# The filter's spectrum as a stage of its own by way of DRAM, filter rows split for two t at once, scratch ordered by re/im

## The chip, the cores and the metric

One Trainium2 chip, one of its cores. The metric is the device time of one execution in microseconds. In a core TensorE (PE, with its weight loads as PEld) multiplies matrices into PSUM; VectorE (DVE), ScalarE (ACT) and GpSimd (POOL) do the elementwise work; SyncE (SP) issues most DMAs here, POOL those of the weights and of the constants. The core has 16 DMA engines. Every engine works its own queue in order and waits for others on semaphores.

## The reference

Two branches of the same normalised input are added to it, with S = 2048, D = 576, Dff = 4608, all in float32:

```python
def _A_ref(q, k, v, shift_k, ssm_k, ssm_D):
    ...
    for t in range(ks):                       # ks = 4
        k_shift = k_shift + k_pad[:, t:t + S, :] * shift_k[:, ks - 1 - t][None, None, :]
    kv = k_shift * v
    ...
    y_f = kv_f * kf_f[None, :, :, :]          # FFT of length 2 S over the sequence, per channel
    y = irfft2(y_f, ...)[:, 0, :S, :]
    y = y + kv * ssm_D[None, None, :]
    return q * y

def _B_ref(x, w1, w2):
    h = jnp.maximum(jnp.einsum("bsd,df->bsf", x, w1), 0)
    return jnp.einsum("bsf,fd->bsd", h, w2)

x = A_q
xn = _layernorm(x, axis=-1)
return x + _A_ref(xn, A_k, A_v, A_shift_k, A_ssm_k, A_ssm_D) + _B_ref(xn, B_w1, B_w2)
```

## The kernel before

**The FFN** is the larger part. It runs over two halves of the sequence (`half`), 12 chunks of 384 hidden columns (`cc`), two blocks of 512 rows (`bi`). For each, three `mm1` (L352) of 14 matmuls with 512 columns make a hidden tile; ACT (`hh`, L367) and DVE (`ll`, L368) evacuate it as a high and a low part. Four `mm2` (L371) of 2 x 9 matmuls with 288 columns follow, added to `acc` by DVE (L389, L393). Every fp32 operand is split into a high and a low part and multiplied in three passes.

**The convolution** is a transform in two steps, 2048 = 64 x 32. It is a Python generator, `conv` (L435), that emits its work in small pieces and yields a cost after each. `tick` (L753) is called twice in every `mm1` and `mm2`, with the FFN's columns as its clock, and lets the next piece be emitted when its credit allows: credit grows by `rate` (L746) times the columns. A negative yield is a pause, in which nothing is emitted until the clock has moved by so much. Thus each engine's queue holds FFN work with convolution work put between, in an order that is fixed when the kernel is built. There, `here()` (L429) ties a piece to the last `acc` and `act` instruction of the FFN, so that it is not put ahead of them.

The stages, each with a tile pool of its own:

- *Filter* (`fk`, L440). The filter is loaded as `kt`, 128 x 288 x 32 (a row holds 32 values of t for each of 288 channels). For each of the 32 columns t2, `prepare` (L460) splits `kt[:, :, t]`, read at a step of 32 elements, into `stk` for two halves of the channels. `first` (L421) multiplies each by a constant, two matmuls of 288 columns, and ACT copies the result to `z`. SP stores `z` to `zk[:, t2, :]` (L480): 128 rows of 2304 B.
- *Signal* (`fx`, L485). The same for k * v after the four taps: 32 stores to `zx` (L557).
- *Frequency* (`fm`, L560). For each of 32 groups g, 128 rows of 576 columns are loaded from `zk` and from `zx` (L572), split (L579, L580), and multiplied by the second step's matrix (`run`, L583: three matmuls of 288 columns for each half). Four copies build the filter's real and imaginary part in `k1` and `k2` (L610 to L613), two build the swapped signal `sw`; DVE multiplies and adds; the product is split again, multiplied by the inverse matrix and stored to `zy` (L648).
- *Output* (`fo`, L651). 32 loads from `zy` (L663, 128 rows each), split, the inverse of the first step, the gate with q, and the sum with `acc` (or with `fin`, the first half's result).

The scratch tensors are [128, 32, 576]: 64 x 2 frequencies and parts, t, channels. The rows that a group reads are one contiguous block. `rate` is `FFT_TOTAL`, the sum of the costs, over the FFN's columns times `SHARE` less `PAUSES` pauses. `turned_xT` (L280) turns the second half's rows for the FFN by way of `xv`, two buffers.

```python
def halves(u):
    return slice(u * A1, (u + 1) * A1), slice((1 - u) * A1, (2 - u) * A1)
```

Of the kernel before, what the change touches and what calls it, by code (L numbers as in the profile page):

```python
# [10 lines left out]
F32 = mybir.dt.float32  # L11
# [37 lines left out]
PAUSES = 16  # L49
# [7 lines left out]
FFT_TOTAL = N_FK * W_FK + N_FX * W_FX + N_FM * W_FM + N_FO * W_FO  # L57
# [18 lines left out]
def transform_constants():  # L76


    p1 = np.arange(A1)[:, None]
    f1 = np.arange(A1)[None, :]  # L80
    fwd = np.zeros((T, 2, A1, U, 2, A1, 2), np.float32)
    inv = np.zeros((T, A1, 2, U, 2, A1), np.float32)
    for t in range(T):
        for u in range(U):
            phi = 2 * np.pi * (A2 * p1 + T * u + t) * (f1 - 0.25) / S
            for c, m in enumerate((np.cos(phi), -np.sin(phi))):
                hi, lo = _split12(m)
                fwd[t, :, :, u, 0, :, c] = hi
                fwd[t, :, :, u, 1, :, c] = lo
                hi, lo = _split12(m.T / S)  # L90
                inv[t, :, c, u, u, :] = hi
                inv[t, :, c, u, 1 - u, :] = lo

    a = np.zeros((GR, 2, A2, 2, GR, A2))
    th = 2 * np.pi * np.arange(A2)[:, None] * np.arange(A2)[None, :] / A2
    for r in range(GR):
        a[r, 0, :, 0, r, :] = np.cos(th)
        a[r, 1, :, 0, r, :] = np.sin(th)
        a[r, 0, :, 1, r, :] = -np.sin(th)
        a[r, 1, :, 1, r, :] = np.cos(th)  # L100
# [8 lines left out]
def h3_ffn_kernel(ctx: ExitStack, tc, x, k, v, shift_k, ssm_k, ssm_D, w1, w2, fwd, inv, mid, out):  # L109
# [20 lines left out]
    zx = dram.tile([P, A2, D], F32, name="zx")  # L130
    zk = dram.tile([P, A2, D], F32, name="zk")
    zy = dram.tile([P, A2, D], F32, name="zy")
# [147 lines left out]
    def turned_xT(b):  # L280
# [4 lines left out]
        for c0 in range(0, 5, 2):  # L285
# [148 lines left out]

    def conv():  # L435
# [4 lines left out]
        with tc.tile_pool(name="fk", bufs=2) as fp:  # L440
            kt = fp.tile([P, NH, A2], F32, tag="kt", name="kt", bufs=1)
            skip = fp.tile([P, NH], F32, tag="skip", name="skip", bufs=1)
# [17 lines left out]
            def prepare(t, h):  # L460
                stk = fp.tile([P, NH], F32R, tag="stk", name=f"ks{t}_{h}", bufs=5)
                with here():
                    stack(stk, kt[:, :, t], h)
                return stk

            order = [T * u + t for t in range(T) for u in range(U)]
# [4 lines left out]
            for n, t2 in enumerate(order):  # L471
                stk, nxt = nxt, []
                u, t = divmod(t2, T)
                z = fp.tile([P, D], F32, tag="z", name=f"zk{t2}")
                for h in range(2):
                    first(ws[t], stk[h], z[:, h * NH:(h + 1) * NH], u)
                    if n + 1 < len(order):
                        nxt.append(prepare(order[n + 1], h))
                    yield W_FK
                nc.sync.dma_start(zk[:, t2, :], z)  # L480
                if u == U - 1 and t + 2 < T:
                    ws[t + 2] = load_const(fp, fwd[t + 2], f"wk{t + 2}")


        with tc.tile_pool(name="fx", bufs=2) as fp:  # L485
# [54 lines left out]
            for t in range(T):  # L540
# [7 lines left out]
                for u in range(U):  # L548
# [8 lines left out]
                    nc.sync.dma_start(zx[:, T * u + t, :], z)  # L557


        with tc.tile_pool(name="fm", bufs=2) as fp:  # L560
            m_sb = fp.tile([P, 2, 2, P], F32R, tag="m", name="m_sb", bufs=1)
            nc.gpsimd.dma_start(m_sb, mid)

            def rows(z, g):
                return z[g * 2 * GR:(g + 1) * 2 * GR].rearrange("q t d -> (q t) d")

            raw, parts = {}, {}

            def load(z, g, name):
                if g < NG:  # L570
                    raw[name, g] = fp.tile([P, D], F32, tag="zt", name=f"zt{name}{g}", bufs=3)
                    nc.sync.dma_start(raw[name, g], rows(z, g))  # L572

            def split(name, g):
                if g < NG:
                    hi = fp.tile([P, D], F32R, tag="hi", name=f"hi{name}{g}", bufs=4)
                    lo = fp.tile([P, D], F32R, tag="lo", name=f"lo{name}{g}", bufs=4)
                    with here():
                        nc.scalar.activation(hi, raw[name, g], AF.Copy)  # L579
                        nc.vector.tensor_tensor(lo, raw[name, g], hi, OP.subtract)  # L580
                    parts[name, g] = hi, lo

            def run(hi, lo, d, h):  # L583

                ps = fft_psum()
                cols = slice(h * NH, (h + 1) * NH)
                seq = [(m_sb[:, d, 0, :], hi), (m_sb[:, d, 0, :], lo), (m_sb[:, d, 1, :], hi)]
                for n, (a, m) in enumerate(seq):
                    nc.tensor.matmul(ps[:, :NH], a, m[:, cols], start=n == 0, stop=n == 2)  # L589
                return ps[:, :NH], cols  # L590

            load(zk, 0, "k")
            load(zx, 0, "x")
            yield -PAUSE
            for name, z in (("k", zk), ("x", zx)):
                split(name, 0)
                load(z, 1, name)
                yield -PAUSE / 8


            pend = back = None
            for g in range(NG + 1):
                if g < NG:
                    k1 = fp.tile([P, D], F32, tag="k1", name=f"k1_{g}")
                    k2 = fp.tile([P, D], F32, tag="k2", name=f"k2_{g}")
                    sw = fp.tile([P, D], F32, tag="sw", name=f"sw{g}", bufs=1)
                for h in range(2):
                    if g < NG:
                        ps, cols = run(*parts["k", g], 0, h)
                        nc.scalar.activation(k1[:64, cols], ps[:64], AF.Copy)  # L610
                        nc.scalar.activation(k1[64:, cols], ps[:64], AF.Copy)  # L611
                        nc.scalar.activation(k2[:64, cols], ps[64:], AF.Copy, scale=-1.0)  # L612
                        nc.scalar.activation(k2[64:, cols], ps[64:], AF.Copy)  # L613
                    if h == 0 and pend is not None:
                        yh, p1 = pend
                        yl = fp.tile([P, D], F32R, tag="yl", name=f"yl{g - 1}")
                        nc.vector.tensor_tensor(yl, p1, yh, OP.subtract)
                        back = yh, yl
                    yield W_FM
                if g < NG:  # L620
                    for h in range(2):
                        ps, cols = run(*parts["x", g], 0, h)
                        nc.scalar.activation(sw[:64, cols], ps[64:], AF.Copy)
                        nc.scalar.activation(sw[64:, cols], ps[:64], AF.Copy)
                        nc.vector.tensor_tensor(k1[:, cols], ps, k1[:, cols], OP.mult)
                        if h == 0:
                            split("k", g + 1)
                            load(zk, g + 2, "k")
                        yield W_FM
                if back is not None:  # L630
                    vo = fp.tile([P, D], F32, tag="vo", name=f"vo{g - 1}")
                for h in range(2):
                    if back is not None:
                        ps, cols = run(*back, 1, h)
                        nc.scalar.activation(vo[:, cols], ps, AF.Copy)
                    if g < NG:
                        if h == 0:
                            nc.vector.tensor_tensor(k2, sw, k2, OP.mult)  # L638
                            split("x", g + 1)
                            load(zx, g + 2, "x")  # L640
                        else:
                            nc.vector.tensor_tensor(k1, k1, k2, OP.add)  # L642
                            yh = fp.tile([P, D], F32R, tag="yh", name=f"yh{g}")
                            nc.scalar.activation(yh, k1, AF.Copy)
                            pend = yh, k1
                    yield W_FM
                if back is not None:
                    nc.sync.dma_start(rows(zy, g - 1), vo)  # L648


        with tc.tile_pool(name="fo", bufs=2) as fp:  # L651
# [101 lines left out]
    def tick(cost):  # L753
# [6 lines left out]
        if clock["conv"] < 0:  # L760
            return
        try:
            c = next(stream)
        except StopIteration:
            clock["done"] = True
            return
        if c < 0:
            clock["until"] = clock["ffn"] - c
        else:
# [95 lines left out]
```

## Time and profile before

| what | us |
|---|---|
| median of 3 runs (1074.35 to 1075.35) | 1074.39 |
| the profiled execution's own time | 1077.91 |
| its span | 1076.1 |
| PE / DVE / ACT / POOL busy | 1065.8 / 742.7 / 584.3 / 322.9 |

The span runs from the first instruction of the profiled execution to its last; the rest of that execution's time lies around it. A window row gives its length, then each engine's busy time and number of instructions, the granted clock, the mean busy share of the 16 DMA engines and GB/s. A row of a group gives busy time, mean ns of one, and the engine's idle time before it with what ended that. A row of the DMA view gives the number of issues, the size of one, and the median time from issue to landing. A packet is one piece of a DMA on one of the engines.

### The profile page before, as it was taken

Reading aid. Unit: us, or ns where it says so; the run is one execution under the profiler, and the core shown is the slowest. Engines: PE = TensorE matmul, PEld = TensorE weight load, DVE = VectorE, ACT = ScalarE, POOL = GpSimd, SP = SyncE. Lnnn points to the kernel's source line nnn. Section 1 sums busy time; section 2 is a strip of 40 time slices with the busy share of each in tenths; the row PEclk is TensorE's granted clock in tenths of the full one; section 3 lists DMA queues with packets and bytes.
Section 4 is the critical chain, followed back from the end, with each engine's and each line's share of the span. In section 5 each row is a group of like instructions: output and inputs, shape, how many; then the busy total and the mean of one; then the engine's idle time right before and its main releaser. Section 6 shows DMA issues by size and latency. Waiting matters only on the chain.

```text
span 1076.1 us, 17258 instructions
## 1 busy us (share of the span) xinstructions
PE 1065.8 (99%) x6505; PEld 971.1 (90%) x6505; DVE 742.7 (69%) x1225; ACT 584.3 (54%) x1181; POOL 322.9 (30%) x307
## 2 busy tenths in 40 slices
PE   8999999999999999999999999999999999999998
PEld 5989999989999999999999999899999998899998
DVE  6323787849998789876466666666566656877774
ACT  4321787823442422434478788787887865443430
POOL 4341342423423413413413131221313032342410
PEclk9999999999999999999999999999999999999999
DMA  9950455665544438528834251534334127644523
GB/s 228 188 158 1 145 165 167 195 179 153 177 134 151 151 99 259 149 73 212 244 96 158 67 169 66 169 112 124 108 118 147 67 93 233 196 133 135 175 76 110
DMA packets 119342, 155.49 MB, mean 144 GB/s; under 512 B 64397, under 2 KB 68719, under 8 KB 119260
## 3 DMA queue, kind: packets, MB, share of 16 engines
q1 hardware_dynamic: 99708, 97.59, 31.2%
q0 software_dynamic: 19232, 56.08, 17.3%
q8 instruction: 51, 0.84, 0.3%
q10 hardware_dynamic: 320, 0.74, 0.3%
q14 instruction: 31, 0.25, 0.1%
HBM read 116.62 MB, written 37.75 MB: 143 GB/s over the span
## 4 chain that ended last, share of the span: by engine, by line
PE 82%; ACT 6%; DVE 6%; DMA 4%; issue 2%; SPq 1%; ACTq 0%; DVEq 0%
PE pso L385 36%; PE psh L362 36%; PE psf L589 5%; PE psf L425 3%; DMA acc<-in_x 1%; DVE lox L580 1%; DVE k L638 1%; DVE k L642 1%; ACT k L612 1%; DMA sk<-in_shift_k 1%; ACT k L613 1%; ACT k L611 1%; PE psf L727 1%; DMA zo<-zy 1%; PE psf L728 1%
## 5 line engine op out<-in xcount | busy, mean ns | idle before, releaser
L305 POOL TENSOR_TENSOR l<-r,h 128x640 fp32r<-128x640 f32 (+1 forms) x144 | 226.2, 1575 | 525.5 <-ACT h L335 393.7
L385 PE MATMUL pso<-l,hh 128*128 128x288 f32 x1152 | 338.2, 295 | 0.0
L385 PE MATMUL pso<-h,ll 128*128 128x288 f32 x1152 | 337.6, 295 | 0.0
L385 PE MATMUL pso<-h,hh 128*128 128x288 f32 x1152 | 336.5, 295 | 1.1 <-DVE acc L393 0.9
L362 PE MATMUL psh<-xhi,h 128*128 128x512 f32 x576 | 225.9, 393 | 1.6 <-DVE ll L368 1.2
L362 PE MATMUL psh<-xlo,h 128*128 128x512 f32 x576 | 226.2, 393 | 0.0
L362 PE MATMUL psh<-xhi,l 128*128 128x512 f32 x576 | 225.3, 391 | 0.0
L385 PEld LDWEIGHTS pso<-h,hh 128*128 128x128 f32 x1152 | 215.5, 188 | 8.1 <-DVE acc L393 1.6
L385 PEld LDWEIGHTS pso<-l,hh 128*128 128x128 f32 x1152 | 216.0, 188 | 5.7
L385 PEld LDWEIGHTS pso<-h,ll 128*128 128x128 f32 x1152 | 215.7, 188 | 0.4
L367 ACT ACTIVATE hh<-psh 128x512 fp32r<-128x512 f32 x144 | 85.5, 595 | 167.2 <-PE psh L362 162.3
L393 DVE TENSOR_TENSOR acc<-pso,acc 128x288 f32<-128x288 f32 x288 | 128.1, 451 | 64.3 <-PE pso L385 61.6
L368 DVE SCALAR_TENSOR_TENSOR ll<-psh,hh 128x512 fp32r<-128x512 f32 x144 | 98.7, 686 | 101.3 <-ACT hh L367 101.0
L362 PEld LDWEIGHTS psh<-xhi,l 128*128 128x128 f32 x576 | 108.2, 188 | 20.4
L362 PEld LDWEIGHTS psh<-xhi,h 128*128 128x128 f32 x576 | 108.0, 188 | 17.6 <-DVE ll L368 1.4
L362 PEld LDWEIGHTS psh<-xlo,h 128*128 128x128 f32 x576 | 108.1, 188 | 15.2 <-DVE xlo L205 0.4
L344 ACT ACTIVATE h<-r 128x576 fp32r<-128x576 f32 x72 | 48.6, 681 | 54.7 <-DMA r<-in_w 29.3
L389 DVE SCALAR_TENSOR_TENSOR acc<-pso,rstd,acc 128x288 f32<-128x288 f32 x96 | 48.3, 511 | 29.3 <-PE pso L385 28.7
L419 DVE TENSOR_TENSOR ks<-kt,ks 64x288 fp32r<-64x288 f32 x64 | 57.8, 903 | 2.2 <-ACT ks L418 0.3
L580 DVE TENSOR_TENSOR lok<-ztk,hik 128x576 fp32r<-128x576 f32 x32 | 28.7, 898 | 41.8 <-ACT hik L579 41.7
L426 ACT ACTIVATE zx<-psf 128x288 f32<-128x288 f32 x64 | 25.7, 407 | 57.3 <-PE psf L425 37.9
L362 PE MATMUL psh<-xhl,l 128*128 128x512 f32 x144 | 56.5, 392 | 0.0
(114 smaller groups left out, 1543.4 us busy)
## 6 DMA issues: line engine op xcount, KB each, us to landing
r<-in_w POOLq DMA_DIRECT2D x23, 864.0 KB, 5.7
r<-in_w POOLq DMA_DIRECT2D x23, 768.0 KB, 5.8
zk<-zk SPq DMA_DIRECT2D x32, 288.0 KB, 2.6
zx<-zx SPq DMA_DIRECT2D x32, 288.0 KB, 3.4
ztk<-zk SPq DMA_DIRECT2D x32, 288.0 KB, 2.9
ztx<-zx SPq DMA_DIRECT2D x32, 288.0 KB, 2.8
zy<-vo SPq DMA_DIRECT2D x32, 288.0 KB, 2.2
zo<-zy SPq DMA_DIRECT2D x32, 288.0 KB, 3.1
```

The costliest lines, as they stand in the source:

```text
L305: return nc.gpsimd.tensor_tensor(dst, src, hi, OP.subtract)
L344: nc.scalar.activation(h2, r2[:, j, :], AF.Copy)
L362: nc.tensor.matmul(ps, a, m, start=i == 0, stop=i == len(seq) - 1)
L367: done["act"] = nc.scalar.activation(hh, ps, AF.Relu)
L368: nc.vector.scalar_tensor_tensor(ll, ps, 0.0, hh, op0=OP.max, op1=OP.subtract)
L385: nc.tensor.matmul(ps[:, :NH], a[:, cols], m[:, dc], start=n == 0, stop=n == 3 * FT - 1)
L389: done["acc"] = nc.vector.scalar_tensor_tensor(acc[t][:, dc], ps[:, :NH], rstd[:, t:t + 1], acc[t][:, dc], op0=OP.mult, op1=OP.add)
L393: done["acc"] = nc.vector.tensor_tensor(acc[t][:, dc], ps[:, :NH], acc[t][:, dc], OP.add)
L419: nc.vector.tensor_tensor(dst[other], src[own], dst[own], OP.subtract)
L425: nc.tensor.matmul(ps[:, :NH], w[:, u, n, :], stk, start=n == 0, stop=n == 1)
L580: nc.vector.tensor_tensor(lo, raw[name, g], hi, OP.subtract)
L589: nc.tensor.matmul(ps[:, :NH], a, m[:, cols], start=n == 0, stop=n == 2)
```

## The change

- The scratch tensors become [2, 32, 2, 32, 576]: part (re/im), t, r, g, channel, where frequency f1 = 32 r + g. The constants are permuted to match. `at_t(z, t)` is one t of both parts: two blocks of 64 rows, 2304 B each row. `chunk(z, n)` is 128 rows (part, t, r) of 512 columns of the 32 x 576 (g, channel): 36 chunks in place of 32 groups.
- Filter: `prepare` splits two neighbouring t at once (64 x 288 x 2), and `first` reads its rows as `stk[h][:, :, i]`, every other element. `z` has three buffers, one of them first used by `skip`.
- A new stage `fs` behind the filter stage: for each chunk load, split, three matmuls of 512 columns, evacuate, store to `spec` in DRAM.
- Frequency: the filter's parts are loaded from `spec`, the real part to both halves of `kr`, the imaginary to both of `ki` (four DMAs of 64 rows a chunk). Three matmuls of 512 columns each way in place of six of 288.
- Signal and output store and load by `at_t`. Costs and `PAUSES` are new; `tick` may emit two pieces at once, and a pause cuts off credit; `xv` has one buffer.

```diff
-PAUSES = 16
+PAUSES = 23
...
-N_FK, N_FX, N_FM, N_FO = 4 * T, 4 * T, 6 * NG, 4 * T
-W_FK, W_FX, W_FM, W_FO = 1.4, 4.1, 1.26, 2.4
+CW = 512
+NCH = NG * D // CW
+N_FK, N_FS, N_FX, N_FM, N_FO = 4 * T, NCH, 4 * T, 2 * NCH, 4 * T
+W_FK, W_FS, W_FX, W_FM, W_FO = 1.06, 1.67, 4.5, 3.24, 2.35
...
-    zx = dram.tile([P, A2, D], F32, name="zx")
...
+    zx, zk, zy = (dram.tile([2, A2, GR, NG, D], F32, name=name) for name in ("zx", "zk", "zy"))
+    spec = dram.tile([NCH, P, CW], F32, name="spec")
...
+    def at_t(z, t):
+        return z[:, t].rearrange("c r g d -> c (r g) d")
+    def chunk(z, n):
+        return z.rearrange("c t r g d -> (c t r) (g d)")[:, n * CW:(n + 1) * CW]
...
-                v = xp.tile([P, 512], F32, tag="xv", name=f"xv{b}_{c}", bufs=2)
+                v = xp.tile([P, 512], F32, tag="xv", name=f"xv{b}_{c}", bufs=1)
...
+    def split2(fp, src, name):
...
+            nc.scalar.activation(hi, src, AF.Copy)
+            nc.vector.tensor_tensor(lo, src, hi, OP.subtract)
...
+    def second(m_sb, hi, lo, d):
+        ps = fft_psum()
+        seq = [(m_sb[:, d, 0, :], hi), (m_sb[:, d, 0, :], lo), (m_sb[:, d, 1, :], hi)]
...
-            order = [T * u + t for t in range(T) for u in range(U)]
+            order = [T * u + t for t in range(0, T, 2) for u in range(U)]
...
+                z = [fp.tile([P, D], F32, tag="z", name=f"zk{t2 + i}", bufs=3) for i in range(2)]
                 for h in range(2):
-                    first(ws[t], stk[h], z[:, h * NH:(h + 1) * NH], u)
...
+                    for i in range(2):
+                        first(ws[t + i], stk[h][:, :, i], z[i][:, h * NH:(h + 1) * NH], u)
+                        if i == 0 and n + 1 < len(order):
+                            nxt.append(prepare(order[n + 1], h))
+                        yield W_FK
+                        if h == 1:
+                            nc.sync.dma_start(at_t(zk, t2 + i), z[i])
...
+        with tc.tile_pool(name="fs", bufs=2) as fp:
...
+            for n in range(3):
+                load(n)
+            yield -PAUSE
...
+            for n in range(NCH):
+                hi, lo = nxt
+                out_s = fp.tile([P, CW], F32, tag="s", name=f"sp{n}")
+                ps = second(m_sb, hi, lo, 0)
+                nc.scalar.activation(out_s, ps, AF.Copy)
+                nc.sync.dma_start(spec[n], out_s)
+                if n + 1 < NCH:
+                    nxt = split2(fp, raw[n + 1], f"s{n + 1}")
+                    load(n + 3)
+                yield W_FS
...
-                    nc.sync.dma_start(zx[:, T * u + t, :], z)
+                    nc.sync.dma_start(at_t(zx, T * u + t), z)
...
+                    for c in range(2):
+                        kc = fp.tile([P, CW], F32, tag=f"k{c}", name=f"k{c}_{n}", bufs=3)
+                        for h in range(2):
+                            nc.sync.dma_start(kc[halves(h)[0]], spec[n, halves(c)[0]])
...
+                    ps = second(m_sb, *parts[n], 0)
+                    nc.scalar.activation(sw[:64], ps[64:], AF.Copy, scale=-1.0)
+                    nc.scalar.activation(sw[64:], ps[:64], AF.Copy)
+                    nc.vector.tensor_tensor(kr, ps, kr, OP.mult)
+                    if n + 1 < NCH:
+                        parts[n + 1] = split2(fp, raw[n + 1], f"x{n + 1}")
+                        load(n + 2)
                     yield W_FM
...
+                    nc.vector.tensor_tensor(yl, prod, yh, OP.subtract)
+                    ps = second(m_sb, yh, yl, 1)
+                    nc.scalar.activation(vo, ps, AF.Copy)
+                    nc.sync.dma_start(chunk(zy, n - 1), vo)
...
-                    nc.sync.dma_start(raw[n], zy[:, T * u + t, :])
+                    nc.sync.dma_start(raw[n], at_t(zy, T * u + t))
...
+        for _ in range(2):
+            if clock["conv"] < 0:
+                return
...
+            if c < 0:
+                clock["until"] = clock["ffn"] - c
+                clock["conv"] = min(clock["conv"], 0.0)
+                return
             clock["conv"] -= c
```

More of the change, by code (lines that the diff above doesn't have):

```diff
@@ L433, in here @@
             yield
+    def split2(fp, src, name):
+        hi = fp.tile([P, CW], F32R, tag="hi", name=f"hi{name}")
+        lo = fp.tile([P, CW], F32R, tag="lo", name=f"lo{name}")
+        with here():
+            nc.scalar.activation(hi, src, AF.Copy)
+            nc.vector.tensor_tensor(lo, src, hi, OP.subtract)
+        return hi, lo
+    def second(m_sb, hi, lo, d):
+        ps = fft_psum()
+        seq = [(m_sb[:, d, 0, :], hi), (m_sb[:, d, 0, :], lo), (m_sb[:, d, 1, :], hi)]
+        for n, (a, m) in enumerate(seq):
+            nc.tensor.matmul(ps, a, m, start=n == 0, stop=n == 2)
+        return ps
     def conv():
@@ L441, in conv @@
             kt = fp.tile([P, NH, A2], F32, tag="kt", name="kt", bufs=1)
[L442 removed]
+            skip = fp.tile([P, NH], F32, tag="z", name="skip", bufs=3)
             for h in range(2):
@@ L562, in conv @@
             nc.gpsimd.dma_start(m_sb, mid)
[L564 to L593, printed above, removed]
-            yield -PAUSE
[L595 to L598, printed above, removed]
@@ L601, in conv @@
[L601 to L618, printed above, removed]
-                    yield W_FM
[L620 to L645, printed above, removed]
```

93 lines of the change are left out of this document (57 added, 36 removed).

## The prediction

> **What bounds the kernel now.** I read the page first: engines, slices, chain.
>
> ```profile
> span 1076.1 us, 17258 instructions
> PE 1065.8 (99%) x6505; PEld 971.1 (90%) x6505; DVE 742.7 (69%) x1225; ACT 584.3 (54%) x1181; POOL 322.9 (30%) x307
> ...
> PEclk9999999999999999999999999999999999999999
> ...
> DMA packets 119342, 155.49 MB, mean 144 GB/s; under 512 B 64397, under 2 KB 68719, under 8 KB 119260
> ...
> PE 82%; ACT 6%; DVE 6%; DMA 4%; issue 2%; SPq 1%; ACTq 0%; DVEq 0%
> ```
>
> TensorE is busy almost throughout, at the full clock. A busy share alone doesn't prove it the limit, as neighbouring matmuls overlap in the records, so next come pitches from the chain of waits, in order of time, and then what TensorE waited for:
>
> ```profile
> 43.52 3.20 PE psh L362 x14
> 46.72 2.38 PE pso L385 x18
> ```
>
> ```profile
> PE psf L727 <- DVE y L730: 1.2, 3, 0.8
> PE psh L362 <- DVE ll L368: 1.2, 1, 1.2
> ...
> PE psf L589 <- DVE k L625: 0.8, 2, 0.6
> PE psf L589 <- ACT k L613: 0.6, 1, 0.6
> ```
>
> 14 matmuls of 512 columns take 3.20 us, 228.6 ns each; 18 of 288 take 2.38 us, 132.2 ns each. The program has 2016 of the first (460.9 us) and 3456 + 960 of the second (583.8 us): 1045 us of 1076, nearly all the rest being the start before the first of them. Waits are a microsecond here and there. So TensorE binds, and the frequency stage can give back no more than its own column time and about 1.4 us of waits.
>
> The last view is the table by windows (us; busy time of PE, PEld, DVE, ACT and POOL; clock; DMA share; GB/s). Behind a 0.7 us window inside one store come the filter, signal, frequency and output stages:
>
> ```profile
> 660.70:661.40 0.70, 0.70 (x6) 0.62 (x5) 0.70 (x2) 0.00 (x0) 0.00 (x0) 1.00 1.00 398
> 115.50:218.90 103.40, 103.40 (x644) 95.50 (x644) 83.66 (x115) 83.49 (x152) 33.97 (x35) 1.00 0.50 161
> 253.80:510.90 257.10, 257.10 (x1556) 234.63 (x1555) 218.34 (x345) 94.95 (x178) 81.80 (x74) 1.00 0.53 153
> 527.80:886.60 358.80, 357.35 (x2238) 330.31 (x2237) 230.44 (x384) 284.34 (x629) 89.71 (x76) 1.00 0.37 121
> 890.00:1040.00 150.00, 148.72 (x900) 135.28 (x900) 110.46 (x191) 66.00 (x130) 48.07 (x53) 1.00 0.55 166
> ```
>
> All sixteen DMA engines busy move 398 GB/s, 24.9 each. In every stage they are about half idle, so today DMA is off the path. That holds only while each transfer is spread over all of them, which is where this change needs a close look.
>
> **The change part by part.** First the pace. The stream of convolution steps is slotted between FFN matmuls by the program's own clock. FFN work of 42,240 units (three mm1, four mm2) takes 3 x 3.20 + 4 x 2.38 = 19.1 us, 0.4527 us per 1000. Walking the old clock tick by tick gives 189.1k units for the 64 filter steps; with their 128 matmuls, 85.6 + 16.9 = 102.5 us, against 103.4 in the window, so the walk can be trusted. The new one gives filter 136.5k (78.7 us), spectrum 118.0k (53.4 + 108 x 0.2286 = 78.1), signal 581.0k (279.9), frequency 464.6k (259.7), output 299.3k units (152.4 us). The end of the stream stays at 98% of the FFN.
>
> *Matmuls.* 576 of 288 columns (76.1 us) become 324 of 512 (74.1 us): -2.1 us, on the path. The waits on psf L589 may go or return: 0, bounds -1.4 to +1.4.
>
> *Filter rows for two t.* Now 64 pairs of a 64x288 copy and subtraction, then 32 pairs of twice the width:
>
> ```profile
> L419 DVE TENSOR_TENSOR ks<-kt,ks 64x288 fp32r<-64x288 f32 x64 | 57.8, 903 | 2.2 <-ACT ks L418 0.3
> L418 ACT ACTIVATE ks<-kt 64x288 fp32r<-64x288 f32 x64 | 47.3, 739 | 4.7 <-DVE kt L458 3.2
> L418 ACT ACTIVATE xs<-c 64x576 fp32r<-64x576 f32 x32 | 21.9, 684 | 34.3 <-DVE c L519 30.9 <-issue 2.9
> ```
>
> ACT drops from 47.3 us to between 21.9 (rows read contiguously, last line) and 47.3; DVE likewise. TensorE covers it, without a gap in that stage (103.40 of 103.40): 0. The filter matmuls then read every other element. Cost between 0 and a doubling, 128 x 132 ns = 16.9 us; the nearest row is the strided copy, 739 ns for half the elements of the 684 ns one, which is a step of 128 B and not of 8. I take 0 and keep the other end for a rival.
>
> *Spectrum stage and frequency stage.* The filter's four small copies a half (L610 to L613) go, 36 evacuations and 36 stores come. ACT and DVE have room: 284 and 230 of 359 us there. On SP's queue each chunk has six issues (zx, four filter pieces, zy) in 7.2 us. The load for n+2 waits for the yl of n-1, whose buffer it takes; behind it queue only zy's store and the next chunk's loads, needed a chunk later. The stage costs 0 while DMA holds: 18.9 MB plus 40 GB/s of weights (the r rows below, 43 MB over the span) is 22 MB in 78 us, 282 GB/s of 398.
>
> *One xv buffer.*
>
> ```profile
> L205 DVE TENSOR_TENSOR xlo<-xv,xhi 128x512 fp32r<-128x512 f32 x8 | 5.2, 682 | 0.2
> L204 ACT ACTIVATE xhi<-xv 128x512 fp32r<-128x512 f32 x8 | 5.0, 634 | 3.0 <-DVE xv L297 3.0
> ```
>
> Ten transposes then wait for the split of the one before; xhi is needed only in the second half of the FFN: 0, at most 2 us.
>
> *Scratch ordered by re/im.* This is the large term. `chunk` still joins to 128 equal rows. `at_t` doesn't: its DRAM side is 2 blocks (re, im) of 64 rows, with the other t between them, so its outermost count is 2 where it was 128. Rows that tell what that does, from the DMA view (first and last of 42 issue rows, whose counts sum to 572, and those of odd shape):
>
> ```profile
> r<-in_w POOLq DMA_DIRECT2D x23, 864.0 KB, 5.7
> r<-in_w POOLq DMA_DIRECT2D x23, 768.0 KB, 5.8
> zk<-zk SPq DMA_DIRECT2D x32, 288.0 KB, 2.6
> zx<-zx SPq DMA_DIRECT2D x32, 288.0 KB, 3.4
> ...
> zo<-zy SPq DMA_DIRECT2D x32, 288.0 KB, 3.1
> kt<-in_ssm_k SPq DMA_DIRECT2D x16, 288.0 KB, 6.4
> ...
> r<-in_w POOLq DMA_DIRECT2D x46, 96.0 KB, 5.6
> ...
> xw<-rows_n SPq DMA_DIRECT2D x36, 64.0 KB, 2.6
> ...
> k-3_2416<-in_k SPq DMA_DIRECT2D x1, 141.8 KB
> k-2_2420<-in_k SPq DMA_DIRECT2D x1, 141.8 KB
> k-1_2424<-in_k SPq DMA_DIRECT2D x1, 141.8 KB
> ...
> skip<-in_ssm_D SPq DMA_DIRECT2D x2, 1.1 KB
> ```
>
> The page counts 64,397 packets under 512 B. kt moves in runs of 128 B, 16 x 2304, and xw too, 36 x 512: 55,296. That leaves 9,101, where 572 DMAs with one closing packet from each of 16 engines would make 9,152: 51 missing. Five DMAs are odd: two of one row, three of 63. If one row runs on 1 engine and 63 rows on 9, then 2 x 15 + 3 x 7 = 51, exactly. So a transfer is dealt out in equal shares of its outermost count, to as many engines, up to 16, as divide it. By that, a count of 2 gives two engines. Such a transfer then drains 294,912 B at 2 x 24.9 GB/s: 5.93 us instead of 0.74, and always on the same two engines if the first ones are taken. 32 of them make 190 us on those two in each of filter (zk), signal (zx) and output (zo).
>
> The Trainium skill, "DMA: Bandwidth & Descriptors", section "Why a DMA increments its semaphore by 16 and not by 1", says that the largest number up to 16 that divides the outermost count of both sides sets the engines, and the lowest-numbered are used; the 9 and the 1 above agree, a 2 is in no run yet. By its rule the sum would be mine.
>
> Other traffic takes the same two engines. *Filter:* 0.50 x 103.4 = 51.7 us per engine, 23.7 of it zk (9.44 MB at 398 GB/s), so 28, some 24 in a shorter stage: 214 us for 78.7 of work. Three z buffers let two stores run ahead; then ACT's copy of psf waits for the store, and behind it in ACT's queue are the FFN's hh, so mm2 starves. Today that wait is 0.5 us in all (what waited for zk, by tile):
>
> ```profile
>   ACT zk L426: 0.5, 2
> ```
>
> What the stores ran ahead by falls due at the spectrum stage, which needs all of zk; only its pause of 16,000 units, 7.2 us, and some buffer slack come off: +125 us (bounds 104, with zk alone on the engines, and 140). *Signal:* 0.53 x 257.1 - 23.7 = 113 us of others, 303 for 279.9: +23 (0 to 45, as k, v and fwd loads queue behind the stores). *Output:* 0.55 x 150 - 23.7 = 59, 249 for 152.4, less three loads issued during the pause: +85 (20 to 100). Here ACT's split waits for zo. Sum: 125 + 23 + 85 - 2 = +231 us. The profiled execution took 1077.91 us, 1.8 over its span and 3.5 over the median of 1074.39: 1078 + 231 - 3.5 = **1305 us**. With all terms at their ends, 1074 + 122 = 1196 and 1074 + 290 = 1364.
>
> **The rivals.** *All sixteen engines after all* (the transfer is cut into more shares than its outermost count): place, every at_t transfer; price, nothing, as 2.46 us per store in the filter stage less 0.75 of other traffic leaves 1.7, which 5.93 x 2 / k meets from 7 engines on. Then the matmul columns decide, less the waits: 1074.4 - 2.1 - 1.4 = 1071 us, faster. For it speaks that nothing in the trace ever has an outermost count of 2; against it, the exact 51. *Sixteen engines, but the new stage binds:* the start, where loads come together, is the worst row:
>
> ```profile
> 0.00:23.00 23.00, 20.02 (x88) 12.08 (x89) 14.33 (x43) 11.21 (x20) 10.97 (x15) 1.00 0.96 219
> ```
>
> At 219 / 0.96 = 228 GB/s the 22 MB need 97 us instead of 78; or the strided operand costs its 16.9: 1071 + 17 to 19, about 1089 us. Against it: the 398 of the clean window. *The change doesn't deliver:* sixteen engines, and the 2 us of columns come back as waits, since the spectrum's chain (copy, split, subtraction: by L204 and L205 0.63 + 0.63 + 0.68 us) nearly fills the 2.2 us between its matmuls: 1074 us.
>
> **How the numbers follow.** Two engines 0.82, at 1305 us, its own range 1180 to 1390: the ends of the sum, with room for transfers on the other queues that are held up behind these. Sixteen and hidden 0.11; sixteen and bound 0.04; no gain 0.03. That range leaves out the three rivals and a sliver of the first case, 2 in 10. About 0.2% (2 us) can be told from no change here: faster 0.10, within it 0.04 (the last rival and a little of the second case), slower 0.86.
>
> **What would show it.** Landings of zk, zx and zo of 7 us and more, not 2.6 to 3.4; 96 x 14 closing packets fewer than sixteen each; ACT zk waiting on DMA zk for 100 us, ACT ohi on DMA zo for some 80, PE near 82% busy, gaps in the filter and output stages and few in frequency. If zk lands in under 3 us, the forecast falls whole; if it lands in 7 us and the filter stage still takes 80 us, the buffers hide more than I think, and the time would be near 1100.

## The result and the profile after

| | median us | runs | ratio to before (95%) |
|---|---|---|---|
| before | 1075.04 | 5 (1074.35 to 1077.32) | |
| after | 1322.08 | 5 (1320.47 to 1324.42) | 1.2294 (1.2275 to 1.2312) |

The kernel became 247 us slower; the forecast was 1305, range 1180 to 1390. The page of the changed kernel, with the two lines of the chain that ended last:

```profile
span 1320.3 us, 16843 instructions
PE 1153.1 (87%) x6253; PEld 1012.5 (77%) x6253; DVE 702.4 (53%) x1185; ACT 469.1 (36%) x857; POOL 322.4 (24%) x308
PEclk9999979887899998988799999999999988888889
DMA packets 136575, 184.06 MB, mean 139 GB/s; under 512 B 66141, under 2 KB 70463, under 8 KB 136492
PE 45%; DMA 43%; DVE 4%; ACT 4%; issue 2%; SPq 1%; POOL 0%; ACTq 0%; DVEq 0%; POOLq 0%
PE pso L395 19%; PE psh L372 19%; DMA zo<-zy 14%; DMA zk<-zk 13%; DMA zx<-zx 9%; PE psf L459 6%; DMA acc<-in_x 2%; DMA xw<-rows_n 1%; ACT zk L436 1%; DMA fin<-acc 1%; ACT ks L428 1%; DMA xn<-in_x 1%; DVE e L570 1%; PE psf L435 1%; SPq L163 1%
```

DMA held 4% of the chain and holds 43% now, yet the 16 engines move 139 GB/s on average, less than the 144 of before. More time on DMA at a lower mean rate is what transfers look like that use few of the engines. The packet count says how few. 66,141 less the 55,296 data runs of 128 B leaves 10,845 closing packets; 765 DMAs (the 572 of before and 193 more) with 16 each, less the 51 of the odd shapes and less 96 x 14, give 12,240 - 51 - 1344 = 10,845. Each `at_t` transfer closes on 2 engines, to the packet.

How long one takes is in the chain in order of time, here from the middle of the filter stage (start us, us, what):

```profile
184.13 10.47 DMA zk<-zk
...
196.31 10.08 DMA zk<-zk
...
208.13 10.83 DMA zk<-zk
...
220.71 10.47 DMA zk<-zk
```

The chain comes back to a zk store every 12.2 us ((220.71 - 184.13) / 3), and between two such lines two stores are issued: 6.1 us each, against 5.93 predicted. All else between them is ACT's and lasts under 2 us. Who waited, from the table of waits (us, times, longest):

```profile
ACT ohi L703 <- DMA zo<-zy: 137.4, 29, 10.3
ACT zx L436 <- DMA zx<-zx: 132.0, 23, 14.5
ACT zk L436 <- DMA zk<-zk: 121.0, 27, 8.6
ACT his L450 <- DMA zs<-zk: 18.6, 1, 18.6
```

ACT waits in three stages. What ended TensorE's own waits, from the same table:

```profile
PE psf L747 <- DVE y L750: 49.7, 13, 6.8
...
PE psf L435 <- ACT zk L436: 30.8, 15, 5.1
...
PE psf L435 <- DVE xs L429: 19.1, 4, 12.1
...
PE pso L395 <- ACT hh L377: 0.2, 1, 0.2
```

In the filter and output stages TensorE mostly stands at a matmul of the convolution, in the signal stage about half of its waiting time. In the filter stage that matmul waits for `psf`, which ACT's copy `zk` has to empty first; in the output stage for `y`, which waits in turn for ACT's `low`. The FFN's matmuls stand behind it in TensorE's queue. The table by windows shows where (the filter stage, the wait before the spectrum, then spectrum, signal, frequency and output; columns as before):

```profile
117.40:310.40 193.00, 157.76 (x755) 134.75 (x755) 56.13 (x92) 62.50 (x124) 34.34 (x37) 0.89 0.26 84
310.40:332.00 21.60, 5.20 (x26) 3.93 (x24) 2.05 (x4) 2.59 (x5) 3.05 (x4) 0.66 0.30 103
332.00:444.40 112.40, 112.16 (x607) 98.85 (x608) 48.94 (x83) 54.32 (x97) 29.25 (x26) 0.97 0.63 206
472.70:767.00 294.30, 241.99 (x1316) 213.71 (x1317) 204.47 (x328) 87.54 (x170) 81.15 (x72) 0.91 0.49 142
783.60:1047.30 263.70, 263.70 (x1488) 234.22 (x1487) 187.04 (x302) 145.13 (x248) 71.36 (x60) 1.00 0.59 182
1060.00:1295.00 235.00, 179.08 (x945) 158.04 (x944) 116.20 (x204) 69.99 (x136) 48.62 (x53) 0.87 0.34 104
```

Spectrum and frequency, whose transfers are by `chunk` and `spec`, have no gap, at the highest DMA shares of the table. The three stages with `at_t` have large gaps at shares of 0.26 to 0.49, and the granted clock falls there. This points to the shape of a transfer rather than to the bytes.

### The profile page after: what moved, and what is told of

Its sections match the earlier page's. It is cut to its first block, busy times and chain, and to the rows that moved or that the text cites. A ratio compares the mean times of both kernels' runs of the same rounds, so it can differ in the third digit from the quotient of the medians.

```text
span 1320.3 us, 16843 instructions
## 1 busy us (share of the span) xinstructions
PE 1153.1 (87%) x6253; PEld 1012.5 (77%) x6253; DVE 702.4 (53%) x1185; ACT 469.1 (36%) x857; POOL 322.4 (24%) x308
## 2 busy tenths in 40 slices
DMA packets 136575, 184.06 MB, mean 139 GB/s; under 512 B 66141, under 2 KB 70463, under 8 KB 136492
## 4 chain that ended last, share of the span: by engine, by line
PE 45%; DMA 43%; DVE 4%; ACT 4%; issue 2%; SPq 1%; POOL 0%; ACTq 0%; DVEq 0%; POOLq 0%
PE pso L395 19%; PE psh L372 19%; DMA zo<-zy 14%; DMA zk<-zk 13%; DMA zx<-zx 9%; PE psf L459 6%; DMA acc<-in_x 2%; DMA xw<-rows_n 1%; ACT zk L436 1%; DMA fin<-acc 1%; ACT ks L428 1%; DMA xn<-in_x 1%; DVE e L570 1%; PE psf L435 1%; SPq L163 1%
## 5 line engine op out<-in xcount | busy, mean ns | idle before, releaser
L395 PE MATMUL pso<-h,hh 128*128 128x288 f32 x1152 | 348.4, 305 | 21.5 <-DVE acc L403 13.8
L395 PE MATMUL pso<-l,hh 128*128 128x288 f32 x1152 | 348.6, 304 | 15.6 <-POOL l L315 15.6
L395 PE MATMUL pso<-h,ll 128*128 128x288 f32 x1152 | 347.6, 303 | 0.0
L395 PEld LDWEIGHTS pso<-h,hh 128*128 128x128 f32 x1152 | 225.5, 197 | 36.4 <-DVE acc L403 18.0
L395 PEld LDWEIGHTS pso<-l,hh 128*128 128x128 f32 x1152 | 226.8, 197 | 26.1 <-POOL l L315 16.0
L372 PE MATMUL psh<-xhi,h 128*128 128x512 f32 x576 | 235.8, 410 | 9.6 <-DVE ll L378 9.3
L372 PE MATMUL psh<-xlo,h 128*128 128x512 f32 x576 | 235.1, 408 | 0.0
L372 PE MATMUL psh<-xhi,l 128*128 128x512 f32 x576 | 234.0, 406 | 0.0
L395 PEld LDWEIGHTS pso<-h,ll 128*128 128x128 f32 x1152 | 225.8, 196 | 2.7
L372 PEld LDWEIGHTS psh<-xhi,h 128*128 128x128 f32 x576 | 114.0, 198 | 31.9 <-DVE ll L378 12.4
L372 PEld LDWEIGHTS psh<-xhi,l 128*128 128x128 f32 x576 | 113.4, 197 | 23.0
L372 PEld LDWEIGHTS psh<-xlo,h 128*128 128x128 f32 x576 | 114.0, 198 | 18.4 <-DVE xlo L215 0.4
L429 DVE TENSOR_TENSOR ks<-kt,ks 64x576 fp32r<-64x576 f32 x32 | 27.9, 873 | 107.1 <-ACT ks L428 107.0
L436 ACT ACTIVATE zx<-psf 128x288 f32<-128x288 f32 x64 | 24.6, 407 | 145.3 <-DMA zx<-zx 132.0
L435 PE MATMUL psf<-ks,wk 128*128 128x288 f32 x128 | 43.7, 447 | 33.4 <-ACT zk L436 30.8
L750 DVE TENSOR_TENSOR y<-psf,low 64x288 f32<-64x288 f32 x64 | 28.5, 453 | 82.9 <-ACT low L749 82.1
L436 ACT ACTIVATE zk<-psf 128x288 f32<-128x288 f32 x64 | 25.0, 409 | 129.7 <-DMA zk<-zk 121.0
L703 ACT ACTIVATE ohi<-zo 128x576 fp32r<-128x576 f32 x32 | 21.9, 684 | 137.4 <-DMA zo<-zy 137.4
```

The lines of the kernel that those rows point to most:

```text
L372: nc.tensor.matmul(ps, a, m, start=i == 0, stop=i == len(seq) - 1)
L395: nc.tensor.matmul(ps[:, :NH], a[:, cols], m[:, dc], start=n == 0, stop=n == 3 * FT - 1)
L429: nc.vector.tensor_tensor(dst[other], src[own], dst[own], OP.subtract)
L435: nc.tensor.matmul(ps[:, :NH], w[:, u, n, :], stk, start=n == 0, stop=n == 1)
L436: nc.scalar.activation(z, ps[:, :NH], AF.Copy)
L703: nc.scalar.activation(hi, raw[n], AF.Copy)
```

## The experiments

Theory A: the outermost count of 2 puts each `at_t` transfer on two engines, and that is nearly all of the 247 us. Rivals: the strided operand, the pace, the buffers, or VectorE carry part of it. Ratios are to the kernel before on the same chip.

**Spread the transfers.** In the changed kernel alone, each `at_t` transfer becomes two DMAs of 64 rows, one for each part, so that the outermost count is 64:

```diff
+    def by_part(z, t, tile_, load=False):
+        for c in range(2):
+            a, b = tile_[halves(c)[0]], z[c, t].rearrange("r g d -> (r g) d")
+            nc.sync.dma_start(*((a, b) if load else (b, a)))
...
-                            nc.sync.dma_start(at_t(zk, t2 + i), z[i])
+                            by_part(zk, t2 + i, z[i])
```

> Each at_t transfer is cut into two, one for the real and one for the imaginary rows, 64 rows each; scratch, stages and costs stay as in the changed kernel. If two engines for an outermost count of 2 are the cause, the waits on zk, zx and zo (121, 132 and 137 us of ACT) go nearly to nothing and the time falls from 1322 us to about 1087: 1075 less 2.1 us of matmul columns, plus up to 16 us for the filter matmuls, whose pitch was 256 ns in the changed kernel where 132 is usual. If instead the new order of the rows in DRAM, or the added traffic of the spectrum stage, is the cause, it stays above 1250 us.

As the control, again two DMAs for each transfer, but split by columns, so that the outermost count stays 2:

```diff
+        for h in range(2):
+            d = slice(h * NH, (h + 1) * NH)
+            a, b = tile_[:, d], at_t(z, t)[:, :, d]
+            nc.sync.dma_start(*((a, b) if load else (b, a)))
```

> The control to the one before: each at_t transfer is again cut into two, but by columns, so that each still has an outermost count of 2 (128 rows of 1152 B). If the outermost count decides, this stays near the changed kernel, 1322 us, or grows by some tens of us, since the same bytes go over two engines in smaller rows (51 to 68 ns for a row of 1152 B, against 93 for 2304). If it is the size of a transfer or the number in flight, it falls as far as the cut by parts does, to about 1087.

By parts: 1108.09 us, ratio 1.0291 (1.0274 to 1.0308). By columns: 1345.71 us in one run. Twice as many DMAs don't help; the outermost count does, and it is worth 214 us. In the version by parts ACT's wait for zk is gone, the one for zo is down to 3.1 us, and the one for zx has shrunk from 132.0 us:

```profile
ACT zx L442 <- DMA zx<-zx: 5.8, 3, 2.8
```

Three of its windows (the filter stage without its last 19 us, the end of that stage with most of the spectrum stage, and the signal stage with some us on both sides):

```profile
113.00:230.00 117.00, 117.00 (x643) 103.58 (x642) 55.79 (x82) 58.26 (x110) 33.24 (x34) 1.00 0.47 133
230.00:340.00 110.00, 110.00 (x615) 97.60 (x614) 47.93 (x81) 51.94 (x95) 26.39 (x24) 1.00 0.60 190
376.00:660.00 284.00, 271.11 (x1591) 241.59 (x1590) 238.06 (x374) 104.41 (x195) 85.73 (x77) 0.99 0.64 178
```

Filter and spectrum are full; the signal stage is not. So 31 us against before stay (1108.09 us, where the kernel before took 1076.97 on the same chip), about 20 more than I expected, and I looked for them in two places: inside full windows, where matmuls may be slower, and in the signal stage.

**The count of 4.** Here the scratch is [2, 4 x r, t, ...], so that one t has an outermost count of 4:

```diff
-    zx, zk, zy = (dram.tile([2, A2, GR, NG, D], F32, name=name) for name in ("zx", "zk", "zy"))
+    zx, zk, zy = (dram.tile([2, GR, A2, NG, D], F32, name=name) for name in ("zx", "zk", "zy"))
-        return z[:, t].rearrange("c r g d -> c (r g) d")
+        return z[:, :, t].rearrange("c r g d -> (c r) g d")
```

> The scratch is ordered part, r, t, g, so that the outermost count of an at_t transfer is 4, uncut; the second step's matrix is permuted to match. If the transfer is dealt out to as many engines as divide the outermost count, it drains in 2.97 us on four engines: 95 us a stage, 119 with others in the filter stage against 138 us of TensorE work that lay in it, 208 against 216 in the signal stage, 154 against 153 in the output stage. So all but the last few us are hidden: 1087 to 1105 us. If a count under 16 were always confined to two engines, it stays at 1322.

1161.73 us in one run: the expected time was missed. The page's packets and the waits:

```profile
DMA packets 136767, 184.06 MB, mean 159 GB/s; under 512 B 66333, under 2 KB 70655, under 8 KB 136684
```

```profile
ACT zx L436 <- DMA zx<-zx: 60.2, 14, 10.1
...
ACT zk L436 <- DMA zk<-zk: 33.8, 12, 5.5
...
ACT ohi L703 <- DMA zo<-zy: 16.8, 6, 3.7
```

66,333 - 55,296 = 11,037 = 12,240 - 51 - 96 x 12: four engines, to the packet, as the rule has it. What failed was my price for four. On paper the four engines had just room for a stage's traffic; with two or three buffers in front of them ACT still waited 111 us. A mean load below the stage's length is not enough for a hidden transfer. The times for 2, 4 and 16 engines, 1322, 1162 and 1108 us, stand in the order that theory A wants.

**The stores of zk alone by parts.** zx and zo stay on two engines, so of the edit above this line is all:

```diff
-                            nc.sync.dma_start(at_t(zk, t2 + i), z[i])
+                            by_part(zk, t2 + i, z[i])
```

> The changed kernel with the cut by parts for zk's stores alone. By stage, the changed kernel lost 89 us of TensorE time in the filter stage and behind it, 79 in the signal stage and 81 in the output stage. If the stages' losses are separate, this gives back 89 less the 16 of the strided reads that then show: 1322 - 73 = 1249 us, with the signal and output stages as long as before (294 and 235 us). If freeing one stage only moves the wait to the next, it gives back less than 40.

1239.06 us in one run, 83 less than the changed kernel, where 73 were expected; ACT's waits for zo and zx are what they were (135.6 and 132.7 us). So the losses of the stages add up nearly separately.

**The strided operand.** In the version by parts, `stk` is laid out so that a matmul reads neighbouring elements:

```diff
-                stk = fp.tile([P, NH, 2], F32R, tag="stk", name=f"ks{t2}_{h}", bufs=3)
+                stk = fp.tile([P, 2, NH], F32R, tag="stk", name=f"ks{t2}_{h}", bufs=3)
-                    stack(stk, kt[:, :, t2:t2 + 2], h)
+                    stack(stk.rearrange("p i n -> p n i"), kt[:, :, t2:t2 + 2], h)
-                        first(ws[t + i], stk[h][:, :, i], z[i][:, h * NH:(h + 1) * NH], u)
+                        first(ws[t + i], stk[h][:, i, :], z[i][:, h * NH:(h + 1) * NH], u)
```

> As the cut by parts, and the split filter rows are laid out as 2 x 288 in place of 288 x 2, so that the filter matmuls read neighbouring elements. If the step of 8 B is what gives them their pitch of 256 ns, the pitch is 132 again, and the time is 128 x 0.124 = 16 us below the cut by parts, about 1071 us. If that pitch came from TensorE's clock, which was 0.89 in that stage, the pitch is already 132 in the cut by parts, and this one brings nothing.

1093.76 us, ratio 1.0159 (1.0137 to 1.0182): 14 us came back, not all 31. The instructions of the tile `ks` (ns, least / median / most), by parts with the strided read:

```profile
L441 PE MATMUL psf<-ks,wk x128: 415/434/447, 116.6 to 249.4; 128*128 128x288 f32 x128
L434 ACT ACTIVATE ks<-kt x32: 725/742/757, 112.2 to 240.8; 64x576 fp32r<-64x576 f32 x32
```

and with the contiguous one:

```profile
L441 PE MATMUL psf<-ks,wk x128: 288/294/301, 116.5 to 233.6; 128*128 128x288 f32 x128
L434 ACT ACTIVATE ks<-kt x32: 1262/1282/1312, 112.1 to 226.4; 64x576 fp32r<-64x576 f32 x32
```

A matmul that reads every other float takes 434 ns where it took 294; 128 x 0.14 is 18 us, and the stage from its first to its last such matmul is 15.7 us shorter without it (117.1 for 132.8). In return ACT's copy, whose write is now the strided side, takes 1282 ns in place of 742, off the path. The Trainium skill, "SBUF — State Buffer", section "Specifications (TRN2)", says that two hits on a line of 16 bytes give the full rate; ACT's 742 ns for twice the elements of the old 739 ns copy agree, but TensorE's read, two elements in each 16 bytes, does not.

Two more runs place this cost. The kernel before, with the step of 8 bytes and three `stk` buffers as the change has them:

```diff
-                stk = fp.tile([P, NH], F32R, tag="stk", name=f"ks{t}_{h}", bufs=5)
+                stk = fp.tile([P, NH, 2], F32R, tag="stk", name=f"ks{t}_{h}", bufs=3)[:, :, 0]
```

> The kernel before, with the filter stage's split rows laid out 288 x 2 of which every other element is used, and three buffers of them for five. If a step of 8 B alone halves TensorE's rate, each of the 128 filter matmuls goes from 132 to 256 ns and the time from 1077 to 1093 us. If the pitch of 256 ns needed something of the changed kernel, it stays at 1077.

1100.12 us, ratio 1.021 (1.019 to 1.023), 7 us more than expected; with three buffers but no step, a run further down, the ratio is 1.0098, so the step is worth some 12 us in the old kernel. And the changed kernel, on its two engines, with the three edits for the contiguous read and nothing else:

> The changed kernel with the split filter rows laid out 2 x 288 so that TensorE reads neighbouring elements, and nothing else; stores stay on two engines. If the filter stage's length is set by the two engines (214 us of their time from its first store to the spectrum stage's start), the 16 us that TensorE saves are hidden: 1322 us, within 4. If TensorE's own time still counts there, it falls to 1306.

1320.15 us in one run, against 1322.08: a full 16 us of TensorE's work in the filter stage cost nothing there, since the stores set its length. The same operand is dear as soon as they don't. So with the contiguous read on both sides the spread of the transfers is worth not 214 but 226 us (1320.15 to 1093.76, on two chips).

**The rest, at the start of the signal stage.** With parts and contiguous read, the windows of the signal stage up to 550 us and after it:

```profile
383.00:550.00 167.00, 154.23 (x903) 135.50 (x904) 165.17 (x253) 62.37 (x120) 52.12 (x50) 1.00 0.67 182
550.00:618.00 68.00, 68.00 (x411) 61.93 (x410) 45.05 (x76) 26.55 (x49) 25.45 (x22) 1.00 0.63 175
```

VectorE is busy 165 of 167 us while TensorE has its gaps, and TensorE is full once VectorE is not. Its queue holds the taps of the convolution and the FFN's `acc` in one order. Theory B: the change packs the stage's work too densely. First, a slower pace:

```diff
-W_FK, W_FS, W_FX, W_FM, W_FO = 1.06, 1.67, 4.5, 3.24, 2.35
+W_FK, W_FS, W_FX, W_FM, W_FO = 1.06, 1.67, 5.4, 2.9, 2.2
```

> As the cut by parts with unit stride, with other costs only: signal 5.4 for 4.5, frequency 2.9 for 3.24, output 2.2 for 2.35, so that 240 us of FFN work lie in the signal stage as in the kernel before (238), where 198 lay. If the signal stage lost its 20 us because VectorE is full there (165 of 167 us busy), the loss goes and the time is 1094 - 18 = 1076 us, less the 2.1 us of matmul columns: 1074 to 1077. If the loss came from DMA in that stage (busy share 0.67), it stays near 1090.

1088.39 us, ratio 1.0103 (1.0082 to 1.0123): a third came back. The start of the stage is as full as before:

```profile
383.00:440.00 57.00, 52.41 (x303) 45.88 (x304) 56.42 (x89) 21.38 (x42) 20.75 (x21) 1.00 0.63 178
```

Second, with the pace of the change, the last of the four taps left out (16 multiplications and 16 additions of VectorE):

```diff
-                if t >= T:
+                if t >= T or n == KS - 1:
```

> As the cut by parts with unit stride, but the last of the four taps is left out, 16 multiplications and 16 additions of 128x576 on VectorE (about 29 us of it); the order on TensorE is nearly the same. If VectorE binds the signal stage, the time falls from 1094 to 1074 to 1079 us. If DMA does, it stays at 1090 to 1094.

1087.45 us in one run: 6 us came back, not some 17. VectorE is as full at the start (55.87 of 57 us). Less of its work in the stage doesn't thin the start; something else is put there. Third, the pace of the slower run, and the second half's normalisation, which is VectorE work too, emitted three chunks earlier:

```diff
-                if half == 0 and cc == NCHUNK - 3:
+                if half == 0 and cc == NCHUNK - 6:
```

> As the run with other costs, and the normalisation of the second half's rows (16 statistics of 128x288 and 8 of 128x576 on VectorE, about 14 us of it, with its loads and stores) is emitted three FFN chunks earlier, beside the spectrum stage, where VectorE was 46% busy. With other costs 15 us were lost between 353 and 520 us, where VectorE was 98 to 99% busy. If VectorE's load at the start of the signal stage is the cause, most of it goes: 1074 to 1079 us. If it is DMA there (busy share 0.63 to 0.74), which this relieves less, it stays above 1083.

1083.91 us, ratio 1.0066 (1.0053 to 1.0078): better than the slower pace alone by less than half of what was expected, and the nearest to the kernel before that I found. Fourth, the kernel before with nothing but three `stk` buffers for five:

```diff
-                stk = fp.tile([P, NH], F32R, tag="stk", name=f"ks{t}_{h}", bufs=5)
+                stk = fp.tile([P, NH], F32R, tag="stk", name=f"ks{t}_{h}", bufs=3)
```

> The kernel before with three buffers for the split filter rows in place of five, nothing else. In the order that this gives TensorE, 99 us of FFN work lie in the filter stage for 85. If that shift is what puts the signal stage's start on the FFN chunks whose statistics and turns also need VectorE, the time grows by the 6 to 10 us that the run with a step of 8 B lost behind the filter stage: 1083 to 1087 us. If those were the strided reads' too, it stays within 2 us of 1077.

1086.13 us, ratio 1.0098 (1.0081 to 1.0115), as expected. Here two windows from the end of the filter stage on, then the same stretch with five buffers:

```profile
234.00:270.00 36.00, 31.95 (x181) 28.84 (x180) 20.81 (x35) 7.30 (x13) 9.69 (x11) 0.95 0.69 195
270.00:330.00 60.00, 57.29 (x343) 51.38 (x343) 59.09 (x83) 24.19 (x46) 18.22 (x17) 1.00 0.50 152
```

```profile
218.90:253.90 35.00, 34.15 (x202) 30.62 (x202) 22.79 (x35) 8.78 (x14) 13.85 (x12) 1.00 0.67 196
253.90:310.00 56.10, 56.10 (x342) 51.12 (x341) 53.06 (x78) 22.68 (x43) 13.90 (x14) 1.00 0.51 153
```

Three buffers cost the old kernel 10 us without any of the rest of the change, and its gaps are in the same place: TensorE is idle for 6.8 us of these two windows, with five buffers for 0.9. Last, then, the best version with the old filter stage: one t at a time, five buffers, and the pace adjusted to it:

```diff
-PAUSES = 23
+PAUSES = 21
...
-W_FK, W_FS, W_FX, W_FM, W_FO = 1.06, 1.67, 5.4, 2.9, 2.2
+W_FK, W_FS, W_FX, W_FM, W_FO = 1.4, 1.67, 5.0, 3.0, 2.35
...
-                stk = fp.tile([P, 2, NH], F32R, tag="stk", name=f"ks{t2}_{h}", bufs=3)
+                stk = fp.tile([P, NH], F32R, tag="stk", name=f"ks{t}_{h}", bufs=5)
...
-            order = [T * u + t for t in range(0, T, 2) for u in range(U)]
+            order = [T * u + t for t in range(T) for u in range(U)]
```

> The spectrum stage and the 512-column pieces, with at_t transfers cut by parts, the early normalisation, and the filter stage as in the kernel before: one t at a time, five buffers for the split rows. In the built order 79 us of FFN work lie in the filter stage and 255 in the signal stage, after 100 and 234. If the three buffers, by pushing FFN work forward, are what costs the 8 us that are left, these go and the columns' 2 us show: 1073 to 1077 us, at the kernel before or just under it. If the signal stage is still full on VectorE where it begins, 1080 to 1084.

1085.82 us, ratio 1.009 (1.0074 to 1.0107): missed. The filter stage has its old length back, but the gap behind it stays. What TensorE and VectorE waited for between 335 and 460 us, and the chain there:

```profile
PE pso L401 <- DVE acc L405: 6.0, 3, 3.9
```

```profile
DVE e L573 <- DMA k-1_3478<-in_k: 7.8, 1, 7.8
```

```profile
344.34 12.45 DMA k-2_3474<-in_k
...
356.81 5.35 DMA k<-in_k
```

The signal stage's first loads are issued right behind the spectrum stage's last stores and take up to 12.45 us; VectorE's tap waits for them, with the FFN's `acc` behind it. The old kernel's tap waits there too, 5.3 us, with a gap of 0.9 us on TensorE; with three buffers, and in the versions by parts, that wait is 5.1 to 7.8 us, whatever the gap. So that the loads make the gap is argued, not shown: loads issued earlier were not tried, and these last 8 to 10 us stay open. Theory B is borne out in part only: the slower pace and the earlier normalisation gave back 10 us together, the left-out tap and the five buffers less than it asked. No version beat the kernel before.

## Why the prediction held, and where it didn't

**The count of 2, two engines, 5.93 us a transfer.** Right on all three: the packets are exact, the pairs come every 12.2 us, and 2, 4 and 16 engines stand in order. The Trainium skill's rule in "DMA: Bandwidth & Descriptors", section "Why a DMA increments its semaphore by 16 and not by 1", of which no run had shown a 2, holds for 2 and for 4 by these counts.

**The wait that passes it on to TensorE.** Half right. ACT's copy does wait for the store, 121.0 us. But then I had `mm2` starve for the `hh` behind that copy in ACT's queue, and waits that `hh` ended are 0.2 us of TensorE's; those that ended with `ll`, which follows `hh`, are 9.3. TensorE stopped at the convolution's own matmuls, 30.8 us for `zk` and 49.7 us for `y`. The total didn't suffer: in the filter stage the stores set the length, as the run with contiguous reads alone shows.

**The stages' lengths.** Right for the three stages with `at_t`. I had 211 us for the filter up to the spectrum (79 + 125 + the pause of 7), 303 for the signal and 237 for the output. Measured: 214.6 (117.4 to 332.0), 294 and 235. Frequency, at 263.7 for 259.7, has no gap. The drain on two engines was well priced. The spectrum stage was not right: 112.4 us (332.0 to 444.4), forecast 78.1.

**The terms +125, +23, +85.** Two of them were wrongly sized, in opposite directions. A stage's loss is its length less the work in it. Of the FFN's matmuls, mm1 (L372) and mm2 (L395) in the filter, the spectrum and the signal stage there were:

```profile
117.40:332.00 214.60, 70.39 (x239) 0.87 0.26 86
117.40:332.00 214.60, 71.13 (x414) 0.87 0.26 86
332.00:444.40 112.40, 49.95 (x190) 0.97 0.63 206
332.00:444.40 112.40, 50.78 (x310) 0.97 0.63 206
472.70:767.00 294.30, 116.93 (x432) 0.91 0.49 142
472.70:767.00 294.30, 121.94 (x756) 0.91 0.49 142
```

At the pitches of 228.6 and 132.2 ns that is 109 us of FFN work in the filter stage, 84 in the spectrum stage and 199 in the signal stage. The walk of the pacing clock had put 62, 53 and 263 there (78.7, 78.1 and 279.9 less the stage's own matmuls). With 16.9 us of filter or signal matmuls in each, the losses are 214.6 - 109 - 17 = 89 and 294.3 - 199 - 17 = 79; the output's comes to 81 in the same way. Sum 249, less the columns' 2: 247, as measured. The error of 36 in the filter and of 56 in the signal stage nearly cancel, as FFN work that covers one stage is missing in another. That is why the total was only 17 us off, and it wasn't foreseen: so close a sum is in part luck. What doesn't cancel is work that ran in the spectrum stage, which had no gap to cover. The upper end of the sum adds up to 140 + 45 + 100 - 2, 1357 us, and not to 1364; nothing hangs on it.

The step that failed is "so the walk can be trusted". I had checked the walk on the old kernel, with five `stk` buffers. The two runs that have three and wait for no store show the difference: filter matmuls from 115.6 to 231.6 us in the old kernel with three buffers, where five gave 115.6 to 218.2, and 116.6 to 233.7 in the version with parts, contiguous read and early normalisation, though its pace for the stage is a quarter faster (1.06 for 1.4). With three buffers the stage holds about 100 us of FFN work at either pace. Which rule of the built order does that, the runs don't show. Nor are the buffers all of it: with five of them, in the last run, the spectrum stage lasts 112 us too (226.0 to 338.3).

**The strided operand: 0, other end 16.9.** The other end was nearly right: 14 us by the ratios of the pair with and without it, 15.7 in the stage. I had chosen the row of ACT's copy, another engine, as the nearest. In the result it doesn't appear, as the run with contiguous reads alone shows.

**Filter rows for two t.** ACT's 64x576 copy takes 733 ns, 23.4 us in all, near the low end of 21.9 to 47.3; hidden, as said.

**The spectrum stage and the frequency stage at 0.** Right: windows without a gap, and in the version by parts too, at 190 GB/s.

**What would show it.** ACT's wait for zk: about 100 forecast, 121.0 measured; for zo 80 and 137.4, more than TensorE loses there, since TensorE still has work while ACT waits. TensorE was to be busy near 82% and is at 87%, but with the clock at 0.87 to 0.91 in the stalled stages its matmuls are longer, so the share says too much. The landings of 7 us can't be read: the DMA view gives none for these transfers.

**The 31 us behind the two engines** were not in the sum: 14 of stride, and about 17 more, with the gaps around the start of the signal stage. Three buffers alone cost the old kernel 10; in the new one five didn't bring them back, and pace and early normalisation gave back 10.

## What to carry to other kernels

Before a scratch layout is changed, look at the outermost dimension of both sides of every transfer that uses it: a leading 2 for re and im left a transfer two of the sixteen engines here, 6.1 us for a store, and two DMAs of 64 rows undid that. A change of buffer count in one stage can move other work between stages, so a pace tuned with one count needs to be tested again with another. A cost that is hidden behind a larger one (here the strided operand) has to be measured with the larger one removed.

## What the runs showed of the hardware

- A DMA of 288 KB with an outermost count of 2 or 4 on its DRAM side closed on 2 or 4 of the 16 engines; on 2, a store took 6.1 us.
- TensorE's moving fp32r operand at a step of 8 bytes: 434 ns for 288 columns, 294 contiguous. ACT, reading pairs of floats 128 B apart, took 742 ns for 576 columns, near the 684 of a contiguous copy.
- The same copy written in turns to two places 1152 B apart: 1282 ns.
- Mean granted clock 0.66 in the window where TensorE was busy 5.20 of 21.60 us, 1.00 in the frequency stage, where it was busy 263.70 of 263.70 us.
